# Plain first products in the first block, weight combinations made in the second, and a late half that begins with the weights at hand

## The chip, the core and the metric

The kernel runs on one core of a Trainium2 chip. A core has TensorE (PE; PEld is its weight load), VectorE (DVE), ScalarE (ACT), GpSimd (POOL) and SyncE (SP), which take their instructions in order and wait for one another by semaphores. Here SP issues nearly all loads and POOL the stores. The metric is the device time of one execution in microseconds (us); lower is better.

## What is computed

```python
for t in range(S):                                   # attention: 4 batches, 8 heads, 768 steps, head 64
    state = gamma * state + einsum('bhd,bhe->bhde', k[:, :, t], v[:, :, t])
    y[:, :, t] = scale * einsum('bhd,bhde->bhe', q[:, :, t], state)
x = y.transpose(0, 2, 1, 3).reshape(3072, 512)
h = x @ w_in                                         # layer 0: 512 -> 2048 -> 512
x = np.maximum(0.01 * h, h) @ w_out
h = np.maximum(x @ w_in2, 0.0)                       # layer 1, same sizes
return (h * h) @ w_out2
```

All is float32; weights arrive as 64-bit words and are turned into float32 on the core.

## The kernel before

**Attention.** The 768 steps are three chunks of 256. A unit is one batch and one pair of heads in one chunk: 16 units a chunk. A unit's scores (`sc`) go through a mask on DVE (`pm`), then give its outputs (`y`, copied into `xs` by ACT) and the state's update (`sp`). Chunk 0 runs ahead of everything; one unit of a later chunk is put into each iteration of the early halves and into each of the first steps of the late halves of blocks 0 and 1.

**Layers.** The 3072 rows make three blocks of 1024 per layer: blocks 0, 1, 2 in layer 0 and 3, 4, 5 in layer 1, one after another. A block's 1024 rows are two tiles of 512 columns (t = 0, 1). Each block has an early half with 8 iterations q, which makes the hidden values of both tiles for 256 hidden features per iteration and the second matmuls of tile 0, and a late half, which makes the second matmuls of tile 1 from kept hidden values (`g1`).

**First products.** `emit_in` uses Strassen's scheme as Winograd writes it: the 2x2 block product of weights (`wa`, `wb`: seven combinations) and operands (`xh`, `xl`: seven combinations) takes 7 products instead of 8, at the price of additions on DVE. Every float32 factor is a pair, high and low part, so a product is 6 matmuls of 512 columns (high x high, low x high, high x low, for two halves of the contraction): 42 per iteration. The sums that a product leaves go through ACT (L369 copies, L374 activation) and DVE (L395, L399, L403 add). `split_g` makes the pair `gh`, `gl`.

**Second matmuls.** `emit_out` sends 12 matmuls for each of the 16 slices j of 128 features, into four accumulators, with weights `wo` (two buffers of 1 MB, each for two slices).

**Weights.** In the first block of a layer the weights come raw: `load_w` fetches 1 MB into `sg` (two buffers), `cast` (two ACT, three DVE instructions: L239 to L245) makes float32 in `wf`; `make_in` forms the combinations (L269 to L272), splits them into pairs (`wa`, `wb`) and has POOL store them to DRAM (`wid`), `make_out` the same for `wo` (`wod`). Later blocks read them back (`read_in`: 1 MB and 0.75 MB, `read_out`: 1 MB). In block 2 the odd q of layer 1 are made ahead.

**Order.** Matmuls, loads (SP) and stores (POOL) keep the order of the code. A scheduler at build time sets the order on ACT and DVE by its own estimate of times. PSUM has four accumulators (`ps_acc`), three buffers for products and scores together (`ps_h`), and one for `y`.

Of the kernel before, what the change touches and what calls it, by code (L numbers as in the profile page):

```python
# [40 lines left out]

UNIT = {7: 0, 4: 1, 2: 2, 1: 3, 5: 4, 6: 5, 3: 6}
# [3 lines left out]
def retention_then_two_mlps(  # L46
# [44 lines left out]
    ups = [(c * B + b, p) for c in range(NC) for p in range(NP) for b in range(B)]  # L91
# [128 lines left out]
    wod = {}  # L220
    ydr = {}
    for lay in range(2):
        for q in range(NQ):
            wid[lay, q] = dram.tile([P, 2 * 7 * 256], F32, name=f"wid{lay}_{q}")
            wod[lay, q] = dram.tile([P, 2 * 1024], F32, name=f"wod{lay}_{q}")
    for b in range(NB):
        ydr[b] = dram.tile([P, KB, TB], F32, name=f"ydr{b}")
# [21 lines left out]
    def in_tiles(lay, b, q):  # L249
        ta, tb, bufs = "wa", "wb", (1, 1)  # L250
        pool = w_p
        if q % 2 and late:
            pool = late["p"]
        elif q % 2 and lay == 0 and b == 1:
            ta, tb, bufs = "sg", "wf", (2, 1)
        a = pool.tile([P, 2, 4, 256], F32R, tag=ta, name="wa", bufs=bufs[0])
        c = pool.tile([P, 2, 3, 256], F32R, tag=tb, name="wb", bufs=bufs[1])
        return a, c
# [6 lines left out]
    def make_in(lay, q, ahead=False):  # L265
        load_w(lay, q, 0)
        f = w_p.tile([P, 7, 256], F32, tag="wf", name="wf", bufs=1)
        cast(stage.pop((lay, q, 0)), f[:, 1:5].rearrange("p n c -> p (n c)"))
# [4 lines left out]
        if ahead:  # L273
            a = late["p"].tile([P, 2, 4, 256], F32R, tag="ea", name="ea")
            c = late["p"].tile([P, 2, 3, 256], F32R, tag="eb", name="eb")
        else:
            a, c = in_tiles(lay, 0, q)
        for t, s in ((a, f[:, 3:7]), (c, f[:, 0:3])):
            nc.scalar.copy(t[:, 0], s)
            nc.vector.tensor_tensor(out=t[:, 1], in0=s, in1=t[:, 0].bitcast(F32), op=ALU.subtract)  # L280
# [11 lines left out]
    def get_in(lay, b, q):  # L292
        if b == 0 and (lay == 0 or q % 2 == 0):
            make_in(lay, q)
# [86 lines left out]
    def emit_in(lay, b, q):  # L381
# [7 lines left out]
        late_g = g_p.tile([P, 2, T], F32, tag=f"t{q}", name="g", bufs=1)  # L389
        c22 = g1[j1] = keep(pd, late_g[:, 1])  # L390
        yield
        product(lay, b, q, 6, pa, False, True)
        c12 = g1[j0] = keep(pa, late_g[:, 0])
# [6 lines left out]
        act_sbuf(lay, c22, True)  # L400
        pb = ps_h.tile([P, T], F32, tag="h", name="pb")
# [12 lines left out]


# [3 lines left out]
    halves = {}  # L419

    def split_g(g, tag=None):
# [6 lines left out]
        nc.scalar.copy(gh, g)  # L428
        nc.vector.tensor_tensor(out=gl, in0=g, in1=gh.bitcast(F32), op=ALU.subtract)  # L429
        return gh, gl  # L430

    def emit_out(lay, b, t, j, gg, first=0, end=12):
        if j == 0 and first == 0:
# [3 lines left out]
        gh, gl = gg  # L437
        passes = ((0, gh), (1, gh), (0, gl))
        if j in (0, NJ - 1):
# [3 lines left out]
        for k, m in order[first:end]:  # L443
# [3 lines left out]
                start=j == 0 and k == 0, stop=j == NJ - 1 and k == 2,  # L447
            )

    def evacuate(lay, b, t):  # L450
        ac = acc.pop((lay, b, t))
        dst = ydr[b] if lay == 0 else out[b]
        for m in range(KB):
            if t:
                if m % 2 == 0:
                    yy = g_p.tile([P, 2, T], F32, tag=f"t{4 + m // 2}", name="y", bufs=1)
# [7 lines left out]
            store(out=dst[:, m, t * T:(t + 1) * T], in_=y)  # L464
# [10 lines left out]
    loads_to(1)  # L475
    nc.scalar.dma_start(out=mk[:, 0], in_=mask[:, 0])
    nc.scalar.dma_start(out=vt, in_=vtab)
    loads_to(4)
    nc.scalar.dma_start(out=mk[:, 1], in_=mask[:, 1])
    n0 = B * NP  # L480
    for n in range(n0 + 1):
        if n < n0:
            loads_to(min(n + 5, n0))
            if n in (4, 8):
                nc.scalar.dma_start(out=mk[:, n // 4 + 1], in_=mask[:, n // 4 + 1])
        attend(n0)
        if n == 3:
            make_in(0, 0)
        elif n == 7:
            make_out(0, 0)  # L490
        elif n == 9:
            steps = operands(0, 0)
            next(steps)
            next(steps)
    for _ in steps:
        pass
# [7 lines left out]
    def put_out(lay, b, j):  # L504
        emit_out(lay, b, 0, j, halves.pop(j))

    def split_late(j):
        halves[j] = split_g(g1.pop(j), f"t{j // 2 - 1}" if j % 2 and j > 1 else None)
# [4 lines left out]
    for lay in range(2):  # L513
        for b in range(NB):
# [4 lines left out]
            for q in range(NQ):  # L519
                part = emit_in(lay, b, q)  # L520
                next(part)
                if q:
                    put_out(lay, b, 2 * q - 2)
                next(part)
                if q and q + 1 < NQ:
                    emit_out(lay, b, 0, 2 * q - 1, halves[2 * q - 1], 0, 4)
                if rest:
                    score_next(rest)
                if q and q + 1 < NQ:
                    emit_out(lay, b, 0, 2 * q - 1, halves.pop(2 * q - 1), 4, 12)  # L530
                for _ in part:
                    pass
# [7 lines left out]
                if lay == 0 and b == NB - 1 and q % 2:  # L540
                    make_in(1, q, True)
# [4 lines left out]
            read_out(lay, 0)  # L546
# [3 lines left out]
            read_out(lay, 1)  # L550
            split_late(0)
            split_late(1)
            for j in range(NJ):
                if j + 2 < NJ:
                    split_late(j + 2)
                emit_out(lay, b, 1, j, halves.pop(j))
                if j % 2 == 1 and j + 3 < NJ:
                    read_out(lay, j // 2 + 2)
                if rest and j < 9:
                    attend(rest)  # L560
                if not last and j == 8:
                    steps = operands(nl, nb)
                if not last and j >= 8:
                    next(steps, None)
# [70 lines left out]
```

## Time and profile before

| what | value |
|---|---|
| median of 3 runs | 1198.77 us (1196.65 to 1200.88) |
| the profiled execution | 1199.87 us, its span 1198.1 us |
| busy over the span: PE, PEld, DVE, ACT, POOL | 95%, 74%, 50%, 43%, 4% |
| DMA | 274.57 MB, 229 GB/s in the mean |
| TensorE clock granted, mean | 0.986 of full |

The busy share of PE is counted from modelled ends of matmuls, so it hides short gaps. What tells is the distance between starts, and a comparison of equal stretches of work: the early halves of blocks 0 and 1 send the same matmuls, and so do those of blocks 2 to 5 among themselves, and all late halves of blocks 2 to 5.

### The profile page before, as it was taken

The page shows a single profiled execution, that of the slowest core. Times are in us where ns is not written, and L with a number is a line of the kernel's source. Part 1 is how long each engine was busy: PE and PEld are TensorE (multiplying, and loading weights), DVE is VectorE, ACT ScalarE, POOL GpSimd, SP SyncE. Part 2 cuts the span into 40 slices and gives each one's busy share as a digit, 9 for nine tenths or more (in the row PEclk, how much of TensorE's full clock was granted, in tenths as well). Part 3 has the DMA queues.
Part 4 walks back from the last instruction along what each step waited for, and adds up shares of the span by engine and source line. Part 5 has one row for each costly group of instructions (what it writes and reads, how often), then busy time and mean ns, then how long its engine had stood idle before and what let it go on. Part 6 is the DMA issues. An engine that isn't in the chain of part 4 may idle for free.

```text
span 1198.1 us, 13684 instructions
## 1 busy us (share of the span) xinstructions
PE 1139.0 (95%) x5354; PEld 887.3 (74%) x5354; DVE 598.8 (50%) x875; ACT 515.1 (43%) x812; POOL 52.2 (4%) x100
## 2 busy tenths in 40 slices
PE   8798889999999999999988999999999999999996
PEld 5466666767777776788866878777888878888875
DVE  5986776655222344423486387784233372333331
ACT  3755555423333342244564276763233451433430
POOL 0000000000000000000001010000000000000000
PEclk9979999999999999999999999999999999999998
DMA  9657656755645445578748688856746555755263
GB/s 374 250 204 269 245 219 224 250 204 187 230 177 220 171 162 190 214 247 333 310 178 325 233 319 312 314 201 229 286 185 262 193 177 181 276 194 195 82 213 134
DMA packets 50271, 274.57 MB, mean 229 GB/s; under 512 B 6176, under 2 KB 8224, under 8 KB 26784
## 3 DMA queue, kind: packets, MB, share of 16 engines
q1 hardware_dynamic: 38448, 212.88, 48.6%
q0 software_dynamic: 10752, 58.73, 12.3%
q10 hardware_dynamic: 1008, 2.11, 0.5%
q8 instruction: 42, 0.69, 0.2%
q14 instruction: 21, 0.17, 0.0%
HBM read 214.97 MB, written 58.72 MB: 228 GB/s over the span
## 4 chain that ended last, share of the span: by engine, by line
PE 38%; issue 36%; DMA 13%; DVE 8%; ACT 2%; POOL 1%; SPq 0%; ACTq 0%; POOLq 0%; DVEq 0%
PE acc L83 19%; DMA sg<-w 10%; PE pa L83 8%; PE pd L83 4%; PE y L83 3%; PE sc L83 2%; DMA wo<-wod 2%; PE pb L83 2%; POOL out L89 1%; DVE of L242 1%; DMA mk<-mask 1%; DVE g L395 1%; DMA wb<-wid 1%; DVE wf L242 1%; DVE of L245 1%
## 5 line engine op out<-in xcount | busy, mean ns | idle before, releaser
L83 PE MATMUL acc<-gh,wo 128*128 128x512 f32 x1200 | 313.7, 395 | 11.6 <-DMA wo<-wod 11.0
L83 PEld LDWEIGHTS acc<-gh,wo 128*128 128x128 f32 x1200 | 223.2, 189 | 66.9 <-issue 13.0
L83 PE MATMUL acc<-gl,wo 128*128 128x512 f32 x600 | 171.5, 394 | 0.1
L429 DVE TENSOR_TENSOR gl<-g,gh 128x512 fp32r<-128x512 f32 x150 | 101.7, 689 | 112.8 <-PE acc L83 79.1
L83 PEld LDWEIGHTS acc<-gl,wo 128*128 128x128 f32 x600 | 114.2, 190 | 24.9 <-DVE gl L429 0.6
L83 PE MATMUL pa<-xh,wb 128*128 128x512 f32 x384 | 121.9, 399 | 8.9 <-DVE g L399 6.8
L428 ACT CAST gh<-g 128x512 fp32r<-128x512 f32 x150 | 91.3, 620 | 88.7 <-PE acc L83 85.8
L83 PE MATMUL pa<-xh,wa 128*128 128x512 f32 x384 | 121.5, 398 | 7.2 <-ACT g L369 3.7
L83 PE MATMUL pd<-xh,wa 128*128 128x512 f32 x384 | 120.5, 395 | 4.2 <-ACT g L409 3.0
L83 PE MATMUL acc<-gg,wo 128*128 128x512 f32 x504 | 122.2, 391 | 0.0
L395 DVE TENSOR_TENSOR g<-g,pd 128x512 f32<-128x512 f32 x48 | 33.0, 688 | 164.5 <-PE pd L83 138.5
L83 PEld LDWEIGHTS acc<-gg,wo 128*128 128x128 f32 x504 | 94.2, 188 | 20.2 <-issue 0.7
L369 ACT COPY g<-pa 128x512 f32<-128x512 f32 x96 | 56.4, 587 | 121.3 <-PE pa L83 121.1
L374 ACT ACTIVATE g<-g 128x512 f32<-128x512 f32 x72 | 45.3, 631 | 115.7 <-DVE g L399 65.5
L83 PEld LDWEIGHTS pa<-xh,wb 128*128 128x128 f32 x384 | 71.7, 190 | 30.7 <-DVE g L399 12.3
L83 PEld LDWEIGHTS pa<-xh,wa 128*128 128x128 f32 x384 | 71.1, 189 | 24.3 <-ACT g L369 5.4
L83 PEld LDWEIGHTS pd<-xh,wa 128*128 128x128 f32 x384 | 71.8, 189 | 22.8 <-ACT g L409 5.1
L83 PE MATMUL pa<-xl,wa 128*128 128x512 f32 x192 | 75.6, 394 | 1.8 <-DVE xl L325 1.8
L83 PE MATMUL pa<-xl,wb 128*128 128x512 f32 x192 | 75.6, 394 | 0.0
L83 PE MATMUL pd<-xl,wa 128*128 128x512 f32 x192 | 75.3, 392 | 0.0
L399 DVE TENSOR_TENSOR g<-g,pa 128x512 f32<-128x512 f32 x48 | 32.9, 686 | 71.7 <-PE pa L83 71.6
L83 PE MATMUL pb<-xh,wb 128*128 128x512 f32 x192 | 60.0, 394 | 0.0
(77 smaller groups left out, 1280.3 us busy)
## 6 DMA issues: line engine op xcount, KB each, us to landing
wo<-wod SPq DMA_DIRECT2D x80, 1024.0 KB, 4.8
wa<-wid SPq DMA_DIRECT2D x36, 1024.0 KB, 7.1
sg<-w SPq DMA_DIRECT2D x32, 1024.0 KB, 8.9
wb<-wid SPq DMA_DIRECT2D x36, 768.0 KB, 6.4
wod<-wo POOLq DMA_DIRECT2D x16, 1024.0 KB, 5.6
r<-first SPq DMA_DIRECT2D x48, 256.0 KB, 3.6
wid<-wa POOLq DMA_DIRECT2D x12, 1024.0 KB, 8.3
wid<-wb POOLq DMA_DIRECT2D x12, 768.0 KB, 4.6
```

The lines of the kernel that those rows point to most:

```text
L83: tc.keep_in_program_order(nc.tensor.matmul(**kw))
L89: tc.keep_in_program_order(nc.gpsimd.dma_start(**io))
L242: nc.vector.scalar_tensor_tensor(out=ru, in0=hi, scalar=0x80000000, in1=ru, op0=ALU.bitwise_and, op1=ALU.bitwise_or,)
L245: nc.vector.tensor_tensor(out=ru, in0=ru, in1=lo, op=ALU.add)
L369: nc.scalar.copy(t, ps)
L374: nc.scalar.activation(out=g, in_=g, func=AF.Lrelu)
L395: nc.vector.tensor_tensor(out=c12, in0=c12, in1=pd, op=ALU.add)
L399: nc.vector.tensor_tensor(out=c22, in0=c22, in1=pa, op=ALU.add)
L428: nc.scalar.copy(gh, g)
L429: nc.vector.tensor_tensor(out=gl, in0=g, in1=gh.bitcast(F32), op=ALU.subtract)
```

## The change

- **Block 0** makes its hidden values by plain products (`emit_plain`: 8 products of 6 matmuls, 48 per iteration), straight from the four blocks of the weights (`plain_in`, which casts, splits 4 units instead of 7, and stores the float32 blocks, 0.5 MB, to `wraw`). An activation goes directly from PSUM. The units of chunk 0 are ordered so that tile 0 is complete after 8 units; the two products of q = 0 for tile 0 stand among the last units.
- **Block 1** reads `wraw` (0.5 MB) in place of `wid` and makes the combinations there (`make_in` with lay = 0), storing `wid` for block 2.
- **Layer 1** makes q = 0, 1, 3, 5 ahead (in block 2) and q = 2, 4, 6, 7 in block 3.
- **Late halves** begin with q = 6 and 7 (`LATE`), whose `wo` are still there; the reloads start with q = 0.
- **`emit_in`** has six of the twelve matmuls of slice 2q-1 between its products 7 and 2, and six ahead of the scores, where before four stood ahead and eight behind them.
- **Operand steps** of the next block are spread over the late half, each held behind the latest split.
- The masks 1 to 3 are loaded by SP, and the last outputs are stored by SP.

```diff
+LATE = (6, 7, 0, 1, 2, 3, 4, 5)
+AHEAD = (0, 1, 3, 5)
...
+    ups = [(b, p) for t in range(2) for p in range(NP) for b in (2 * t, 2 * t + 1)]
+    ups += [(c * B + b, p) for c in range(1, NC) for p in range(NP) for b in range(B)]
...
+    def pair_up(t, s):
+        nc.scalar.copy(t[:, 0], s)
+        nc.vector.tensor_tensor(out=t[:, 1], in0=s, in1=t[:, 0].bitcast(F32), op=ALU.subtract)
+
+    def plain_in(q):
+        load_w(0, q, 0)
+        f = w_p.tile([P, 4, 256], F32, tag="wf", name="wf", bufs=1)
+        cast(stage.pop((0, q, 0)), f.rearrange("p n c -> p (n c)"))
+        a = w_p.tile([P, 2, 4, 256], F32R, tag="wa", name="wa", bufs=1)
+        pair_up(a, f)
+        store(out=wraw[q], in_=f.rearrange("p n c -> p (n c)"))
+        win[0, q] = a
+
+    def make_in(lay, b, q, ahead=False):
...
+        if lay == 0:
+            load(out=mid, in_=wraw[q])
+        else:
+            load_w(lay, q, 0)
+            cast(stage.pop((lay, q, 0)), mid)
...
-        if b == 0 and (lay == 0 or q % 2 == 0):
-            make_in(lay, q)
+        if lay == 0 and b == 0:
+            plain_in(q)
+        elif (lay == 0 and b == 1) or (lay == 1 and b == 0 and q not in AHEAD):
+            make_in(lay, b, q)
...
         act_sbuf(lay, c22, True)
+        yield
         pb = ps_h.tile([P, T], F32, tag="h", name="pb")
...
+    def emit_plain(q, i, t):
+        j = 2 * q + i
+        a = win[0, q]
+        ps = ps_h.tile([P, T], F32, tag="h", name="pa")
+        for kb in range(KB):
+            kh, kt = divmod(kb, 2)
+            unit = 2 * (1 - kh) + i if kh == 0 else 1 - i
+            for k, (l, r) in enumerate(((0, 0), (1, 0), (0, 1))):
+                mm(
+                    out=ps, lhsT=a[:, l, unit, kt * P:(kt + 1) * P], rhs=xop[t, kh][r][:, kt],
+                    start=kb == 0 and k == 0, stop=kb == KB - 1 and k == 2,
+                )
...
+        nc.scalar.activation(out=g, in_=ps, func=AF.Lrelu)
+        if t == 0:
+            halves[j] = split_g(g)
...
-            store(out=dst[:, m, t * T:(t + 1) * T], in_=y)
+            put = load if (lay, b, t) == (1, NB - 1, 1) else store
+            put(out=dst[:, m, t * T:(t + 1) * T], in_=y)
...
+                if lay == 0 and b == 0:
+                    if q:
+                        emit_plain(q, 0, 0)
+                        put_out(lay, b, 2 * q - 2)
+                        emit_plain(q, 1, 0)
+                    emit_plain(q, 0, 1)
+                    score_next(rest)
+                    emit_plain(q, 1, 1)
+                    if ahead:
+                        put_out(lay, b, 2 * q - 1)
...
-            for j in range(NJ):
-                if j + 2 < NJ:
-                    split_late(j + 2)
-                emit_out(lay, b, 1, j, halves.pop(j))
-                if j % 2 == 1 and j + 3 < NJ:
-                    read_out(lay, j // 2 + 2)
...
+            for i in range(NJ):
+                if i + 2 < NJ:
+                    split_late(i + 2)
+                emit_out(lay, b, 1, 2 * LATE[i // 2] + i % 2, (0, 12), i == 0, i == NJ - 1)
+                if i % 2 and i // 2 + 2 < NQ:
+                    read_out(lay, LATE[i // 2 + 2])
```

How the order moves, at three places. On DVE, in an iteration in the middle of block 0's early half, before (`of` is the float32 of second weights, `wf` that of first weights):

```order
L241 TENSOR_SCALAR of<-of 128x1024
L242 SCALAR_TENSOR_TENSOR of<-sg,of 128x1024
L245 ISA of<-sg,of 128x2048
L241 TENSOR_SCALAR wf<-wf 128x1024
L242 SCALAR_TENSOR_TENSOR wf<-sg,wf 128x1024
L245 ISA wf<-sg,wf 128x2048
L395 TENSOR_TENSOR g<-g,pd 128x512
```

and the same place now:

```order
L247 TENSOR_SCALAR wf<-wf 128x1024
L248 SCALAR_TENSOR_TENSOR wf<-sg,wf 128x1024
L247 TENSOR_SCALAR of<-of 128x1024
L251 ISA wf<-sg,wf 128x2048
L248 SCALAR_TENSOR_TENSOR of<-sg,of 128x1024
L483 TENSOR_TENSOR gl<-g,gh 128x512
L251 ISA of<-sg,of 128x2048
L149 TENSOR_TENSOR pm<-sc,mk 128x384 x2
L272 TENSOR_TENSOR wa<-wf,wa 128x1024
```

The addition L395, which reads the product's PSUM buffer `pd` and stood behind both casts, is gone; a split and the masks stand behind them now. On DVE in block 1's early half, where before L395, L146, L399, L403, L118 and two L429 made up an iteration, an iteration is now:

```order
L291 TENSOR_TENSOR wf<-wf 128x256
L292 TENSOR_TENSOR wf<-wf 128x256
L293 TENSOR_TENSOR wf<-wf 128x256
L294 TENSOR_TENSOR wf<-wf 128x256
L272 TENSOR_TENSOR wa<-wf,wa 128x1024
L272 TENSOR_TENSOR wb<-wf,wb 128x768
L418 TENSOR_TENSOR g<-g,pd 128x512
L149 TENSOR_TENSOR pm<-sc,mk 128x384 x2
L422 TENSOR_TENSOR g<-g,pa 128x512
L427 TENSOR_TENSOR g<-g,pb 128x512
```

The six instructions for the next iteration's weights came in ahead of L418 (the old L395), and the first of them waits for the load of `wraw`. On SP, from the end of block 2's early half into its late half, before:

```order
L86 DMA wo<-wod_7_101 128x2048
L86 DMA sg<-w 128x1024 x2
L86 DMA wo<-wod_0_87 128x2048
L86 DMA wo<-wod_1_89 128x2048
L86 DMA wo<-wod_2_91 128x2048
```

and now:

```order
L88 DMA wo<-wod_7_101 128x2048
L88 DMA wa<-wid_0_102 128x2048
L88 DMA wb<-wid_0_102 128x1536
L88 DMA sg<-w 128x1024
L88 DMA wo<-wod_0_87 128x2048
L88 DMA wo<-wod_1_89 128x2048
```

One of the two raw loads became a read of layer 1's first weights; the reload of q = 0 is issued two slices into the late half and is wanted two slices after that.

## Rows read from the trace of the kernel before

**Rows 1.** Stretches: us, busy us (x instructions) per engine, PEclk, DMA share, GB/s

```profile
49.70:224.00 174.30, 153.30 (x688) 109.83 (x686) 128.26 (x185) 96.77 (x136) 11.68 (x22) 0.94 0.60 226
299.30:434.30 135.00, 134.13 (x654) 101.29 (x653) 39.22 (x65) 44.76 (x80) 1.50 (x3) 1.00 0.51 191
507.90:625.80 117.90, 113.19 (x494) 92.02 (x493) 56.70 (x77) 58.64 (x89) 4.59 (x9) 1.00 0.72 274
634.00:687.00 53.00, 47.12 (x193) 38.06 (x192) 22.13 (x31) 15.97 (x24) 3.20 (x6) 0.94 0.72 271
687.00:804.30 117.30, 113.95 (x493) 91.73 (x493) 92.95 (x118) 82.45 (x117) 9.93 (x18) 1.00 0.79 299
812.50:857.30 44.80, 44.02 (x194) 35.85 (x194) 15.00 (x20) 12.46 (x20) 2.22 (x5) 1.00 0.65 224
857.30:969.50 112.20, 111.81 (x494) 92.25 (x493) 43.65 (x60) 49.70 (x82) 1.40 (x3) 1.00 0.57 220
60.00:72.20 12.20, 11.28 (x29) 7.95 (x29) 10.73 (x15) 5.22 (x6) 0.07 (x1) 0.51 0.31 109
```

**Rows 2.** Chain that ended last: start us, us, what

```profile
315.37 2.72 PE acc L83 x12
...
333.05 2.72 PE acc L83 x12
...
604.71 13.08 DMA sg<-w
...
648.83 9.18 DMA wo<-wod
```

**Rows 3.** PE in order of time: start us, us, instruction, [idle before <-releaser]

```profile
117.60 0.70 PE L83 MATMUL pa<-xh,wa 128*128 128x512 f32 x2
...
131.16 0.92 PE L83 MATMUL sc<-r 64*128 64x128 f32 x6 [1.22 <-DVE g L395]
...
140.65 0.71 PE L83 MATMUL pa<-xh,wa 128*128 128x512 f32 x2
...
496.87 2.08 PE L83 MATMUL acc<-gh,wo 128*128 128x512 f32 x8 [1.54 <-DMA wo<-wod]
```

**Rows 4.** SP's queue in order of time, block 0

```profile
132.11 0.81 SPq L86 DMA_DIRECT2D r<-first  x2
133.01 0.86 SPq L86 DMA_DIRECT2D sg<-w  x2
```

**Rows 5.** The tile sg in 60 to 230 us: its loads

```profile
DMA to landing us min/median/max: 6.2/9.3/12.6
```

**Rows 6.** ACT in order of time, block 0

```profile
122.79 1.12 ACT L239 ACTIVATE of<-sg 128x1024 f32<-128x1024 f32 x1 [1.37 <-DMA sg<-w]
```

**Rows 7.** DVE in order of time, block 0

```profile
129.16 1.23 DVE L245 CUSTOM_DVE_ANT_0 wf<-sg,wf 128x2048 uint16<-128x2048 uint16 x1
130.42 0.69 DVE L395 TENSOR_TENSOR g<-g,pd 128x512 f32<-128x512 f32 x1
```

**Rows 8.** Waits of the whole span: us in total, times, longest

```profile
PE acc L83 <- DMA wo<-wod: 11.0, 6, 3.9
...
PE sc L83 <- DVE g L395: 7.4, 9, 1.4
...
PE pa L83 <- DVE g L399: 6.8, 13, 1.7
```

**Rows 9.** Groups by shape: busy us, mean ns | idle before

```profile
L395 DVE TENSOR_TENSOR g<-g,pd 128x512 f32<-128x512 f32 x48 | 33.0, 688 | 164.5 <-PE pd L83 138.5 <-ACT g L369 25.6
...
L280 DVE TENSOR_TENSOR wa<-wf,wa 128x1024 fp32r<-128x1024 f32 x12 | 14.7, 1224 | 5.1 <-ACT wa L279 4.9
...
L269 DVE TENSOR_TENSOR wf<-wf 128x256 f32<-128x256 f32 x16 | 6.7, 421 | 0.2
```

**Rows 10.** DMA issues: KB each, median us to landing

```profile
wo<-wod SPq DMA_DIRECT2D x80, 1024.0 KB, 4.8
...
r<-first SPq DMA_DIRECT2D x48, 256.0 KB, 3.6
```

More of the change, by code (lines that the diff above doesn't have):

```diff
@@ L220, in retention_then_two_mlps @@
     wod = {}
+    wraw = {}
     ydr = {}
@@ L225, in retention_then_two_mlps @@
             wod[lay, q] = dram.tile([P, 2 * 1024], F32, name=f"wod{lay}_{q}")
+    for q in range(NQ):
+        wraw[q] = dram.tile([P, 1024], F32, name=f"wraw{q}")
     for b in range(NB):
@@ L436, in emit_out @@
         o = wout[lay, j // 2]
[L437 removed]
+        gh, gl = halves[j]
         passes = ((0, gh), (1, gh), (0, gl))
[L439 removed]
+        if begin or end:
             order = [(k, m) for m in range(KB) for k in range(3)]
@@ L442, in emit_out @@
             order = [(k, m) for k in range(3) for m in range(KB)]
-        for k, m in order[first:end]:
+        for k, m in order[part[0]:part[1]]:
             l, r = passes[k]
@@ L446, in emit_out @@
                 out=ac[m], lhsT=o[:, l, j % 2, m * P:(m + 1) * P], rhs=r,
-                start=j == 0 and k == 0, stop=j == NJ - 1 and k == 2,
+                start=begin and k == 0, stop=end and k == 2,
             )
+        if part[1] == 12:
+            halves.pop(j)
     def evacuate(lay, b, t):
@@ L474, in retention_then_two_mlps @@
         )
-    loads_to(1)
     nc.scalar.dma_start(out=mk[:, 0], in_=mask[:, 0])
     nc.scalar.dma_start(out=vt, in_=vtab)
-    loads_to(4)
-    nc.scalar.dma_start(out=mk[:, 1], in_=mask[:, 1])
     n0 = B * NP
+    for p in range(1, NP):
+        loads_to(2 * p)
+        load(out=mk[:, p], in_=mask[:, p])
     for n in range(n0 + 1):
[L482 to L485, printed above, removed]
+        loads_to(min(n + 6, n0))
         attend(n0)
-        if n == 3:
-            make_in(0, 0)
-        elif n == 7:
+        if n == 2:
+            plain_in(0)
+        elif n == 5:
             make_out(0, 0)
[L491 to L496, printed above, removed]
+        elif n == 8:
+            split_first(0)
+        elif n in (11, 14):
+            emit_plain(0, (n - 11) // 3, 0)
+    split_first(1)
     nc.scalar.dma_start(out=qt, in_=qtab)
@@ L502, in read_x, with put_out, split_late @@
         load(out=xs[NB + b], in_=ydr[b])
[L504 to L508, printed above, removed]
+    def put_out(lay, b, j, part=(0, 12)):
+        emit_out(lay, b, 0, j, part, j == 0, j == NJ - 1)
+    def split_late(i):
+        j = 2 * LATE[i // 2] + i % 2
+        halves[j] = split_g(g1.pop(j), f"t{LATE[i // 2 - 1]}" if i % 2 and i > 1 else None)
     def get_out(lay, b, q):
```

100 lines of the change are left out of this document (55 added, 45 removed).

## Prediction, made blind

> **What bounds the kernel now.** I read the stretches first, because they set equal work side by side [rows 1]. PE is full at full clock in most of them, so PE's own matmuls bound the kernel, and what can be gained is where a stretch is longer than its twin. The early halves of blocks 0 and 1 send the same matmuls and attention units (49.7 to 224.0 and 299.3 to 434.3 us): 174.3 us against 135.0 us, so block 0 loses 39.3 us. Of blocks 2, 3 and 4 (layer 0's last and layer 1's first two) the early halves take 117.9, 117.3 and 112.2 us: 5.7 and 5.1 us lost in blocks 2 and 3. The late half of block 2 takes 53.0 us, that of block 3 44.8 us, which itself holds a short wait: about 9 us lost.
>
> Then the chain: 12 matmuls take 2.72 us, 0.227 us each, and in block 1 the same 12 come again 17.68 us later (315.37 and 333.05), one iteration in which PE hardly waits [rows 2]. In block 0 the first products of two following iterations start 23.05 us apart (117.60 and 140.65) [rows 3]. Why, three queues show together. A score waits for a PSUM buffer that L395 frees (131.16) [rows 3]. When the scores are through, SP issues the next unit's loads (132.11), and only behind them the two raw weight loads (133.01), since its queue is in order [rows 4]. Such a load lands 6.2 to 12.6 us after its issue [rows 5]; ACT starts on the second when it lands (122.79) [rows 6], DVE ends the casts at 130.4, and L395 stands behind them (130.42) [rows 7]; then the next scores run. That is a ring of load, cast, addition and score: 1.8 us of issues (132.11 to 133.87), 12.6 us, 7.6 us (122.8 to 130.4) and 0.7 us give 22.7 us, close to the 23.05 us measured.
>
> **The change, part by part.**
>
> *Plain products in block 0.* 8 iterations with 6 more matmuls are 48 x 0.227 = 10.9 us added. The iteration becomes 17.68 + 6 x 0.227 = 19.04 us if nothing waits. DVE loses four additions of 0.42 us, the split of `wb` (under 1.22 us) and three additions of 0.69 us, about 4.7 us per iteration [rows 9]. More than that counts that L395 leaves the ring: a product's buffer is now freed by one ACT instruction, and no PSUM buffer that the scores need stands behind a cast on DVE. What is left of the ring is load, cast, free `sg` buffer, next load. From the second landing only the cast of the second weights is still to do (two on ACT, three on DVE, a split between them): by the 7.6 us of both casts I take 6.2 us, so 12.6 + 6.2 + 0.4 = 19.2 us with the slowest landing, even with PE's 19.04 us. Landings should be faster than that, since block 0 stores 0.5 MB of `wraw` in place of 1.75 MB of `wid`. I expect PE to set the pace. What remains: at the handover from attention two casts and splits of the second tile, of which part is uncovered, 3 us (two splits of 1.22 us and a little [rows 9]); per iteration between 0 and the 1.2 us that L395 cost [rows 3], so 0.7 us, seven times: 5 us. Sum: -39.3 + 10.9 + 8 = -20.4 us. Part of the 39.3 us is 12.2 us at a granted clock of 0.51 after the handover, half speed, 1.2 GHz [rows 1]; I take it that the shorter gaps keep the full clock.
>
> *Late halves with resident weights.* PE waited six times for `wo`, 11.0 us [rows 8]. One, 1.5 us, is deep in block 1's late half [rows 3], where unit loads share the queue; I leave it. The other five come at the third or later slice, because the reload of the second pair is issued only when the early half has ended. Now four slices of 2.72 us can run first, and each reload is issued 5.4 us ahead of its use, against a median landing of 4.8 us [rows 10]: -9.5 us. In block 2 the two waits are the 3.9 us one [rows 8] and one of 2 us, yet that half is about 9 us long: its clock was 0.94 [rows 1], so some 3 us come back too. I keep 1 us as lost: -11.4 us.
>
> *Block 2's end and block 3.* Of the two raw loads at the end of block 2's early half, one of which took 13.08 us to land [rows 2], one becomes a read of 1.75 MB. ACT still waits for the other with block 2's copies behind it: of 5.7 us I keep 3: -2.7 us. In block 3, L399's waits (6.8 us over the kernel [rows 8]) should go, as 12 matmuls instead of 6 now cover it; against that two `make_in` follow each other at q = 6 and 7, on a DVE that is busy 93 of 117 us [rows 1]. Of 5.1 us I keep 2.6: -2.5 us.
>
> *Combinations in block 1.* Per iteration DVE gets 4 x 0.42 + two splits, at most 2.4 us: about 4 us on a DVE that is busy 39 of 135 us [rows 1, 9]. The cover is PE's 17.68 us. The danger is not the sum but the order: these instructions stand ahead of L418 (the old L395), and the first waits for the load of `wraw`. SP issues it behind the reload of `wo`, which waits for slice 2q-1; that is 54 matmuls and the scores into the iteration, 13.1 us, and three issues of 0.4 us more, so 3.4 us before the next iteration. From its landing to L418 some 5.1 us of splits pass (four additions, two splits, one cast of about a us); L418 is wanted after 36 matmuls, 8.2 us. So it is free up to a landing of 8.2 - 5.1 + 3.4 = 6.5 us. For 0.5 MB the nearest rows are 3.6 us (0.25 MB) and 4.8 us (1 MB) [rows 10]: free. Above lie the landings of the crowded block 0 [rows 5]. Every us beyond 6.5 costs 7 us. I take 2 us of cost, less 1 us for score waits that six matmuls ahead of the scores now cover: +1.0 us. The Trainium skill (TensorE: Matmul & The Clock Gate, the table at its head) gives ScalarE and VectorE a strictly in-order queue. Rows 7 agree, with L395 at 130.42 behind the cast; by that rule alone L418 must wait for every late load, which is the slower rival below.
>
> *The rest.* The masks move to SP with the same bytes, about 0.4 us of issue each, behind which no matmul waits: 0. The last stores leave SP instead of POOL: between 0 and 1 us, -0.5 us. Operand steps hide behind the late halves as before; their price if uncovered is a cast and a split, about 2.3 us, once per block.
>
> Sum: -20.4 - 11.4 - 2.7 - 2.5 + 1.0 - 0.5 = -36.5 us. Against the profiled execution's 1199.87 us (span 1198.1 us), 1.1 us above the median of the runs, that gives **1163 us**.
>
> **Rivals.**
> - *Raw loads still pace block 0.* If the landing stays at 12.6 us and the casts take the whole 7.6 us, with 1.8 us of issues, the ring is 22.0 us and not 19.7 us: six full iterations, 14 us, **1177 us**. For it speaks the ring of today; against it that less is stored and that `wf` is cast before the second load lands.
> - *Reloads merely move the wait.* A landing of 9.18 us against a window of 5.4 us was one wait in block 2 [rows 2], and each reload still has that window. If all waits come back a slice pair later, 11.4 us stay: **1175 us**. Against it: late halves 3 to 5 had one wait each at most, and that at the start.
> - *The clock falls again at the handover.* 12.2 us at 0.51 cost about 6 us: **1169 us**. The Trainium skill (TensorE: Matmul & The Clock Gate, Part 1) says that the slow state is the default and that activity releases it; rows 1 agree with their 0.51, and by it any longer gap at the handover would give that 1169 us.
> - *Block 1 takes over the ring (slower).* If the `wraw` loads land as the slowest of block 0 did, 12.6 us, L418 is 6.1 us late in seven iterations, scores and loads slide with it: +43 us, **1206 us**. From a landing of 11.7 us on the change loses (36.5 / 7 = 5.2 us beyond 6.5). Against it: block 1 moved 191 GB/s at a DMA share of 0.51 [rows 1] and gets only 0.5 MB more per iteration.
>
> **Chances.** The forecast 0.62, raw loads 0.15, moved waits 0.08, the clock 0.08, block 1 0.05, others 0.02. The range 1152 to 1182 us holds the first four: the low end is the forecast without the 8 us and most of the 3 us kept as lost, the high end the raw-load rival and some 5 us of late landings in block 1. Faster or slower by over 0.3% is about what can be told from no change here: faster 0.93, same 0.02, slower 0.05.
>
> **What the next profile would show.** Right: first products in block 0 some 19 to 20 us apart, that early half at about 148 us (5.4 us of its matmuls stand among the attention units) and full clock; PE's wait for `wo` near 2 us in all; block 1's early half within a few us of 135; block 2's late half near 44. Wrong: ACT's L245 waiting for `sg` with PE idle behind it; DVE's L291 waiting for `wf` loads and PE's scores for L418; waits for `wo` at the fifth slice.

## The result, and the profile after

The changed kernel takes **1162.94 us** (median of 4 runs, 1160.83 to 1164.19), the kernel before 1198.62 us (4 runs, 1196.65 to 1200.88): ratio 0.970, 95% interval 0.9676 to 0.9724. The profiled execution took 1160.83 us, its span 1158.8 us. The forecast was 1163 us, but its terms are less good than its sum. Two executions of the experiments, of 2885.79 us (the kernel with the ahead load first) and 1603.48 us (the one with operand steps not held), lie far above the others of the same kernel and are left out of its median and ratio.

The same stretches as [rows 1], of the profile after:

```profile
56.00:68.00 12.00, 11.06 (x58) 7.51 (x57) 9.65 (x14) 5.68 (x9) 1.07 (x2) 1.00 0.64 209
55.70:199.70 144.00, 143.06 (x710) 108.99 (x710) 88.14 (x121) 71.64 (x95) 8.52 (x16) 1.00 0.54 201
275.00:411.00 136.00, 134.88 (x655) 101.42 (x653) 63.72 (x106) 56.17 (x93) 8.97 (x17) 1.00 0.56 210
484.30:596.80 112.50, 111.92 (x494) 92.23 (x493) 45.73 (x66) 49.90 (x80) 4.63 (x9) 1.00 0.75 288
611.30:658.90 47.60, 45.05 (x193) 36.93 (x192) 25.86 (x31) 19.06 (x27) 3.20 (x6) 0.96 0.67 251
658.90:775.60 116.70, 113.98 (x493) 91.81 (x492) 92.22 (x121) 81.54 (x116) 10.97 (x20) 1.00 0.81 310
```

PE fills block 0's early half now (143.06 of 144.0 us, clock 1.00), and the handover ran at 1.00, 2.4 GHz, where it was 0.51 [rows 1]. PE's waits of over 0.15 us in that half add up to 0.9 us, both at the handover; before they were 21.0 us: 5.3 us for the first operand splits, the rest spread over the iterations, mostly for ACT's copies and activations and for L395 and L399. Between the stretches of block 2 stand 14.5 us (596.8 to 611.3) for three slices, 36 matmuls that were 8.2 us before (625.7 to 633.8): the place that became slower (block 1's early half lost 1.0 us besides).

PE in block 0, the first products of three iterations, against 23.05 us apart in [rows 3]:

```profile
85.56 0.71 PE L85 MATMUL pa<-xh,wa 128*128 128x512 f32 x2
...
105.04 0.71 PE L85 MATMUL pa<-xh,wa 128*128 128x512 f32 x2
...
124.52 0.71 PE L85 MATMUL pa<-xh,wa 128*128 128x512 f32 x2
```

They are 19.48 us apart. Of the waits, the lines that answer to [rows 8]:

```profile
ACT wf L245 <- DMA sg<-w: 21.9, 10, 5.8
...
PE acc L85 <- ACT gh L482: 6.0, 5, 4.7
...
PE acc L85 <- DMA wo<-wod: 3.8, 2, 2.5
```

PE's waits for `wo` fell from 11.0 to 3.8 us; those for ScalarE's split (L482, L428 before) grew from 0.7 to 6.0 us, 4.7 of them in one place. The stages, each from the start of its first matmul to that of the next stage (tail: from the last matmul row's start plus 12 x 0.227 us to the end of the span):

| stage, us | before | after | forecast step | measured step |
|---|---|---|---|---|
| end of block 0's early half, from the span's start | 223.95 | 199.72 | -20.4 | -24.2 |
| block 1 early / late | 134.9 / 65.3 | 135.9 / 65.0 | +1.0 | +0.7 |
| block 2 early | 117.8 | 112.5 | | -5.3 |
| block 2, last three slices | 8.2 | 14.5 | -2.7 (both rows) | +6.3 |
| block 2 late | 53.2 | 47.7 | with the next late halves | -5.5 |
| block 3 early | 117.3 | 116.7 | -2.5 | -0.6 |
| late halves 3, 4, 5 together | 135.1 | 130.9 | -11.4 (with block 2's) | -4.2 |
| block 4 early | 112.2 | 111.5 | 0 | -0.7 |
| tail | 10.4 | 4.7 | -0.5 | -5.7 |
| sum | | | -36.5 | -39.2 |

**The new wait, read in four queues of the changed kernel.** SP, in the last iteration of block 2: the raw load `sg` that is prepared ahead is issued behind 1.75 MB of block 3's weights.

```profile
582.42 0.38 SPq L88 DMA_DIRECT2D wa<-wid  x1
584.72 0.32 SPq L88 DMA_DIRECT2D wb<-wid  x1
585.10 0.47 SPq L88 DMA_DIRECT2D sg<-w  x1
616.89 0.32 SPq L88 DMA_DIRECT2D wo<-wod  x1
```

ACT stands for it, with two Lrelu (L397) and the splits behind it; the last addition (L427) that they need had long run on VectorE:

```profile
595.61 0.69 DVE L427 TENSOR_TENSOR g<-g,pb 128x512 f32<-128x512 f32 x1 [0.67 <-PE pb L85]
```

```profile
600.13 1.12 ACT L245 ACTIVATE wf<-sg 128x1024 f32<-128x1024 f32 x1 [5.82 <-DMA sg<-w]
601.15 1.13 ACT L246 ACTIVATE sg<-sg 128x1024 uint32<-128x1024 uint32 x1
602.16 1.15 ACT L397 ACTIVATE g<-g 128x512 f32<-128x512 f32 x2
```

PE's slice 14 therefore waits for `gh`, and the fifth slice of the late half for `wo`:

```profile
604.36 3.42 PE L85 MATMUL acc<-gh,wo 128*128 128x512 f32 x8 [4.71 <-ACT gh L482]
...
624.84 3.40 PE L85 MATMUL acc<-gh,wo 128*128 128x512 f32 x8 [2.55 <-DMA wo<-wod]
```

The load landed 15.0 us after its issue (585.10 to 600.13), and the prepared slice was stored late, on POOL, together with block 2's result, just ahead of the read of `wo` at 616.89:

```profile
612.22 0.53 POOL L91 DMA_DIRECT2D wid<-ea  x1 [26.66 <-DVE ea L272]
612.74 0.53 POOL L91 DMA_DIRECT2D wid<-eb  x1
613.27 2.15 POOL L91 DMA_DIRECT2D ydr<-y  x4
```

The Trainium skill (TensorE: Matmul & The Clock Gate, the table at its head) gives ScalarE a strictly in-order queue; the row at 602.16 agrees, two instructions that had their data by 596.3 (the end of L427) ran only behind the casts, the first of which waited 5.82 us for its load.

### The profile page after: what moved, and what is told of

Same layout as the page of the kernel before. It is cut to its first block, busy times and chain, and to the rows that moved or that the text cites. A ratio compares the mean times of both kernels' runs of the same rounds, so it can differ in the third digit from the quotient of the medians.

```text
span 1158.8 us, 13722 instructions
## 1 busy us (share of the span) xinstructions
PE 1133.4 (98%) x5402; PEld 891.9 (77%) x5402; DVE 587.6 (51%) x852; ACT 508.2 (44%) x793; POOL 54.2 (5%) x104
## 4 chain that ended last, share of the span: by engine, by line
PE 85%; DMA 9%; DVE 3%; ACT 2%; issue 1%; ACTq 0%; SPq 0%; DVEq 0%
PE acc L85 42%; PE pa L85 23%; PE pd L85 8%; DMA sg<-w 4%; PE y L85 4%; PE pb L85 4%; PE sc L85 3%; DMA wa<-wid 1%; DMA wo<-wod 1%; PE sp L85 1%; DMA gt<-gtab 1%; DVE of L248 1%; DMA wf<-wraw 1%; ACT sg L246 0%; DVE of L251 0%
## 5 line engine op out<-in xcount | busy, mean ns | idle before, releaser
L85 PE MATMUL pa<-xh,wa 128*128 128x512 f32 x576 | 181.2, 395 | 2.3 <-DVE wa L272 1.4
L85 PEld LDWEIGHTS pa<-xh,wa 128*128 128x128 f32 x576 | 106.2, 188 | 28.7 <-ACT g L462 2.3
L482 ACT CAST gh<-g 128x512 fp32r<-128x512 f32 x150 | 91.2, 620 | 67.6 <-PE acc L85 66.8
L85 PE MATMUL pa<-xl,wa 128*128 128x512 f32 x288 | 112.5, 391 | 0.3 <-DVE xl L348 0.3
L85 PE MATMUL pa<-xh,wb 128*128 128x512 f32 x320 | 99.6, 393 | 0.5 <-ACT g L392 0.5
L85 PE MATMUL pd<-xh,wa 128*128 128x512 f32 x320 | 98.7, 390 | 0.0
L418 DVE TENSOR_TENSOR g<-g,pd 128x512 f32<-128x512 f32 x40 | 27.5, 687 | 130.5 <-PE pd L85 122.7
L149 DVE TENSOR_TENSOR pm<-sc,mk 128x384 f32<-128x384 f32 x96 | 49.2, 551 | 33.1 <-PE sc L85 30.8
L397 ACT ACTIVATE g<-g 128x512 f32<-128x512 f32 x48 | 30.2, 631 | 79.0 <-DVE g L422 31.8
L85 PEld LDWEIGHTS pa<-xl,wa 128*128 128x128 f32 x288 | 54.0, 188 | 12.3 <-DVE xl L348 0.7
L85 PE MATMUL pa<-xl,wb 128*128 128x512 f32 x160 | 62.3, 389 | 0.0
L85 PE MATMUL pd<-xl,wa 128*128 128x512 f32 x160 | 62.3, 389 | 0.0
```

What stands on the lines that cost most here:

```text
L85: tc.keep_in_program_order(nc.tensor.matmul(**kw))
L149: nc.vector.tensor_tensor(out=t, in0=sc[h][:, 128:512], in1=mk[:, p, h], op=ALU.mult)
L397: nc.scalar.activation(out=g, in_=g, func=AF.Lrelu)
L418: nc.vector.tensor_tensor(out=c12, in0=c12, in1=pd, op=ALU.add)
L482: mark[0] = nc.scalar.copy(gh, g).ins
```

## The experiments

Twelve runs of eleven kernels. Ratios are to the kernel before on the same chip, with 95% intervals; the changed kernel's is 0.970 (0.968 to 0.972), and 0.001 is 1.2 us. Stages are from the one profiled execution of each kernel. Where an edit leaves a stage alone it still differs a little: block 0's first product starts at 35.5 to 39.1 us, and in the changed kernel, the first experiment and the two of block 1 the last three slices of block 2 take 14.5 to 16.2 us and its late half 47.7 to 48.2 us.

**Last stores on POOL (and on SP in the kernel before).** Edit, in one kernel undone and in the other added:

```diff
-            put = load if (lay, b, t) == (1, NB - 1, 1) else store
-            put(out=dst[:, m, t * T:(t + 1) * T], in_=y)
+            store(out=dst[:, m, t * T:(t + 1) * T], in_=y)
```

> The changed kernel with its last four stores back on POOL, as they were in the kernel before; nothing else differs. The prediction's step (the stores' move is worth 0.5 us, since one transfer takes the same time from either queue) expects about 1163.4 us and a tail, from the last matmul to the end of the span, of some 5 us. The theory read from the two traces (a program whose last transfers were issued by POOL ends some 6 us later, though no transfer is running then) expects 1168 to 1169 us and a tail of about 10.4 us, with every stage before the tail as in the changed kernel.

Measured: 1167.84 us, ratio 0.973 (0.971 to 0.976). Its last matmuls and stores, span 1166.6 us:

```profile
1152.48 2.88 PE L85 MATMUL acc<-gg,wo 128*128 128x512 f32 x12
...
1156.38 0.54 POOL L91 DMA_DIRECT2D out<-y  x1 [0.25 <-DVE y L519]
```

and those of the changed kernel, span 1158.8 us:

```profile
1151.34 2.88 PE L85 MATMUL acc<-gg,wo 128*128 128x512 f32 x12
...
1152.84 2.48 SPq L88 DMA_DIRECT2D out<-y  x4
...
1154.26 0.69 DVE L519 COPY y<-acc 128x512 f32<-128x512 f32 x1 [0.67 <-PE acc L85]
```

The tail is 11.4 us against 4.7.

> The kernel before with its last four stores moved from POOL to SP; nothing else differs. If the end of the program is set by which queue issued last, whatever came ahead of it, the time falls by the same 5 to 6 us as in the changed kernel: about 1193 us, tail 4.7 us. If the short tail of the changed kernel came from something else there (less traffic at the end, an earlier last matmul), this kernel stays at 1198 us, tail about 10 us.

Measured: 1191.48 us, ratio 0.993 (0.991 to 0.996), tail 4.0 us. So the four stores are worth 4.9 us in the changed kernel and 7.8 us in the kernel before by the medians (6.7 and 6.4 us by the tails), and the prediction's 0.5 us is wrong. The transfers are not what differs: the four last stores land 2.5 us (median) after their issue from POOL and 2.1 us from SP. The Trainium skill (DMA: Bandwidth & Descriptors, Issuing engines are not separate DMA queues) says that issuing DMAs from several engines saves only the time of the issue, as all run on the same DMA engines; the landings agree. The longer end of the program is not a matter of the transfers.

**The ahead load issued before block 3's weights.**

```diff
                 elif not last:
+                    if lay == 0 and b == NB - 1:
+                        make_in(1, 0, AHEAD[3], True)
                     get_in(nl, nb, 0)
...
-                if lay == 0 and b == NB - 1 and q % 2:
+                if lay == 0 and b == NB - 1 and q % 2 and q + 1 < NQ:
                     make_in(1, 0, AHEAD[q // 2], True)
```

> The changed kernel with one change of order in the last iteration of block 2: the load of the raw weights that are prepared ahead for layer 1 is issued before the reads of block 3's first weights (1.75 MB) and not behind them. Theory: the load stands on SP behind reads that wait for their buffer and then share the transfer engines, so it lands 15 us after its issue, ScalarE stands 5.8 us for it, and the products of slice 14 wait 4.7 us for their operand; with the load ahead, its landing falls to 6 to 8 us, both waits go, block 2's three last slices fall from 14.5 to about 8.5 us, and the time to about 1157 us. Rival: the transfers as a whole are the limit there, the order only changes which of them is late; then the time stays at 1163 us and the reads of block 3's weights or of the next output weights are late in its place.

Measured: **1151.08 us, ratio 0.960 (0.957 to 0.962)**, the fastest version. SP, ACT and POOL at the same place:

```profile
580.47 0.42 SPq L88 DMA_DIRECT2D sg<-w  x1
580.99 0.38 SPq L88 DMA_DIRECT2D wa<-wid  x1
...
610.17 0.32 SPq L88 DMA_DIRECT2D wo<-wod  x1
```

```profile
588.82 1.12 ACT L245 ACTIVATE wf<-sg 128x1024 f32<-128x1024 f32 x1 [2.68 <-DMA sg<-w]
```

```profile
600.26 0.53 POOL L91 DMA_DIRECT2D wid<-ea  x1 [16.61 <-DVE ea L272]
601.73 0.53 POOL L91 DMA_DIRECT2D wid<-eb  x1 [0.94 <-DVE eb L272]
...
605.73 0.54 POOL L91 DMA_DIRECT2D ydr<-y  x1 [0.25 <-DVE y L519]
```

Its three last slices and its late half, as windows (their border is one matmul early: from start to start they are 8.2 and 43.5 us):

```profile
596.40:604.30 7.90, 7.90 (x36) 6.55 (x35) 4.80 (x7) 5.01 (x9) 1.61 (x3) 1.00 0.38 155
604.30:648.10 43.80, 43.80 (x195) 36.26 (x194) 25.42 (x30) 19.36 (x27) 1.62 (x3) 1.00 0.66 246
```

One load, 4.6 us earlier, lands 8.3 us after its issue instead of 15.0. Slices and late half fall from 62.2 to 51.7 us, more than the 6 us expected: the stores of the prepared slice leave POOL 12 us earlier too, 9.9 us ahead of the read of `wo`, which lands after 4.8 us instead of 7.8.

**Late halves in the old order.**

```diff
-LATE = (6, 7, 0, 1, 2, 3, 4, 5)
+LATE = (0, 1, 2, 3, 4, 5, 6, 7)
...
             put_out(lay, b, NJ - 3)
+            read_out(lay, 0)
...
             evacuate(lay, b, 0)
+            read_out(lay, 1)
```

> The changed kernel with the late halves in the old order again (slices 0 to 15, each beginning with a reload of the first two output weights, read at the places where the kernel before reads them). The prediction's step (late halves with resident weights gain 11.4 us, of which 10.0 are seen in the stage table) expects the late halves to lose about 10 us in all, 5.5 of them in block 2, and some 1172 to 1175 us. Rival: other parts of the change (operand steps behind the splits, raw loads out of the way) brought that gain, and the resident weights only moved the wait to the reloads at the end; then the time stays within 3 us of 1163.

Measured: 1165.47 us, ratio 0.972 (0.969 to 0.974), within the rival's 3 us of the changed kernel. Late halves 3, 4 and 5 are 44.75, 46.22 and 44.68 us, together 135.7: the gain of 4.2 us there is gone, so there the prediction's step holds. But block 2's late half is 48.8 us, 1.1 more than in the changed kernel (0.7 to 1.1 by the spread above) and 4.4 less than before. Most of its gain came from another part.

**Slices 1, 3, 5, 7 prepared ahead, as before.** Edit: `AHEAD = (1, 3, 5, 7)`.

> The changed kernel with the slices of layer 1 that are prepared ahead put back to 1, 3, 5 and 7, as in the kernel before (slice 0 is then made from raw weights at block 2's end, beside slice 7). Theory, after the run with the old order of the late halves: block 2's late half lost 9 us because two slices were prepared at block 2's end, whose loads and 3.5 MB of stores met the reads of output weights; so this kernel gets block 2's late half back to 52 to 53 us from 47.7, its end (three slices and late half together) to 61 us or more, block 3's early half to 117 or more, and 1166 to 1172 us in all. Rival (the prediction's step: the resident weights alone made the late half short): block 2's late half stays at 47 to 48 us and the time within 2 us of 1163.

Measured: 1159.81 us, ratio 0.967 (0.964 to 0.970); the profiled execution took 1165.15 us, the longest of its five, and its block 1, which the edit leaves alone, is 2.2 us longer too. The time expected was wrong, the place right: late half 50.7 us (+3.0), block 3's early half 118.7 us (+2.1). But no 1.75 MB stand ahead of the ahead load here, and the three slices take 8.6 us, not 14.5. Two sets of stores leave, one 3 us before the late half (which begins at 610.35) and one in it:

```profile
607.23 0.53 POOL L91 DMA_DIRECT2D wid<-wa  x1 [18.30 <-DVE wa L272]
...
621.34 0.53 POOL L91 DMA_DIRECT2D wid<-ea  x1 [13.06 <-DVE ea L272]
...
622.38 2.14 POOL L91 DMA_DIRECT2D ydr<-y  x4
```

and the `wo` read at 622.12, 0.8 us behind the second set's first store, lands after 9.1 us and is late:

```profile
631.31 3.75 PE L85 MATMUL acc<-gh,wo 128*128 128x512 f32 x8 [3.78 <-DMA wo<-wod]
```

In the kernel before (late half from 633.84) the same two sets left POOL at 631.84 and 645.41, 2.2 and 3.4 us ahead of a read of `wo`: those issued at 634.03 and at 648.83 [rows 2], which landed after 7.3 and 9.2 us and made PE wait 2.0 and 3.9 us:

```profile
631.84 0.53 POOL L89 DMA_DIRECT2D wid<-wa  x1 [24.41 <-DVE wa L280]
...
645.41 0.53 POOL L89 DMA_DIRECT2D wid<-ea  x1 [12.51 <-DVE ea L280]
...
646.46 2.15 POOL L89 DMA_DIRECT2D ydr<-y  x4
```

**Operand steps not held behind the splits.** Edit: `next(steps, None)` without the two `issue_after`. It was run twice; the profile is from the second.

> The changed kernel without the order that keeps the operand steps behind the splits of the late slices; the steps are still written at the same places, but the scheduler may set them ahead. The prediction priced this at nothing: the operand steps hide behind the late halves, a cast and a split of 2.3 us once per block if one is uncovered. It expects 1163 to 1166 us. Rival: the order behind the splits is what keeps late slices from waiting for a split that stands behind a 1.2 us step on VectorE; without it the late halves lose a wait of 1 to 2 us at several slices, 10 us or more in all, 1173 us.

> The same kernel as the run without the order of operand steps behind the splits, taken once more for an undisturbed profile (that run's time was 5 to 7 us above the changed kernel, its profile was of an execution at a low clock). Theory: late slices wait for a gg split that stands on VectorE or ScalarE behind operand steps of 1.05 to 1.2 us, so the late halves are longer by 5 to 7 us together, some 1168 us. Rival: the steps come so early that they delay the last slices of an early half or the copies of accumulators, and the loss shows there.

Measured: 1168.39 us, ratio 0.975 (0.972 to 0.978), and 1167.41 us in the second run, a single execution. Both expectations were partly wrong. The order is worth some 5 us (4.5 and 5.5), not 0; yet late halves 3 to 5 do not change (130.9 us), so the loss expected from late `gg` splits is not there. It lies in small pieces, the largest in block 2: its stores leave POOL at 615.52, 1.8 us ahead of the read of `wo`, which lands after 10.0 us, and the wait grows from 2.55 to 4.75 us (+2.8 us on the late half):

```profile
627.52 3.75 PE L85 MATMUL acc<-gh,wo 128*128 128x512 f32 x8 [4.75 <-DMA wo<-wod]
```

The rest: block 2's early half +1.3, block 3's early half and last slices +2.6, block 4's early half +0.7, block 1's +0.5 us.

**Old places of the odd output slices.**

```diff
-                        put_out(lay, b, 2 * q - 1, (0, 6))
+                        put_out(lay, b, 2 * q - 1, (0, 4))
...
-                    next(part)
                     if ahead:
-                        put_out(lay, b, 2 * q - 1, (6, 12))
+                        put_out(lay, b, 2 * q - 1, (4, 12))
```

(and no yield between products 7 and 2)

> The changed kernel with the 12 matmuls of an odd output slice split 4 ahead of the scores and 8 behind them, as before, and none between products 7 and 2 (the changed kernel: 6 behind product 3, 6 between products 7 and 2). The prediction gave the new places 2.5 us in block 3 (L399's waits) and 1 us in block 1 (score waits). It expects some 3 to 5 us over the changed kernel, 1166 to 1168 us: additions of product 7 that product 2 or 4 waits for, some 0.5 us each, come back in blocks 1, 2, 3 and 4. Rival: the waits were set by VectorE's other work, not by the cover; then within 1 us per block and 1163 us.

Measured: 1158.31 us, ratio 0.967 (0.963 to 0.970): faster than the changed kernel by 4.6 us (the intervals still touch), by neither theory. The new places gain 1.6 us in block 3 (118.3 against 116.7) and nothing in the early halves of blocks 1, 2 and 4 (within 0.2 us). But the three last slices of block 2 take 8.2 us here, because the scheduler put the cast behind the last Lrelu and a split, with a load that still lands 13.4 us after its issue:

```profile
596.44 0.61 ACT L481 CAST gh<-g 128x512 fp32r<-128x512 f32 x1
597.46 1.13 ACT L245 ACTIVATE wf<-sg 128x1024 f32<-128x1024 f32 x1 [0.41 <-DMA sg<-w]
```

With the version that issues the load first this makes two cures for the stall of the slices: the load earlier, or the waiting cast later on its engine. Only the first cures the late half too: here the stores leave at 608.96, 0.8 us ahead of a read of `wo`, PE waits 3.7 us for it, and that half takes 49.1 us.

**The ring in block 0 opened in the kernel before.** Edit, in `load_pair`: the two loads of a unit from the second chunk on are issued by `store` (POOL), not `load` (SP).

> The kernel before with the loads of the raw attention units from the second chunk on moved from SP to POOL, so that the raw weight loads no longer stand behind them on SP; products, casts and combinations are as before. The prediction's ring (load, cast, addition, score, and back to the load by SP's order) is then open: an iteration of block 0 falls from 23.05 us to between 17.7 and 20.2 us (12.6 us of landing and 7.6 us of casts, if the two buffers still chain), its early half from 174 to 150 to 158 us, and the time to 1177 to 1185 us. Rival: VectorE's own queue (casts and combinations of 10 us ahead of the additions) sets block 0's pace, whatever SP does; then the early half stays above 170 us and the time near 1198. Either way the loads on POOL stand behind stores there, which can cost something in blocks 0 and 1.

Measured: 1185.68 us, ratio 0.988 (0.985 to 0.991). The additions that end the ring's turns:

```profile
127.82 0.69 DVE L395 TENSOR_TENSOR g<-g,pd 128x512 f32<-128x512 f32 x1 [0.43 <-ACT g L369]
...
147.11 0.69 DVE L395 TENSOR_TENSOR g<-g,pd 128x512 f32<-128x512 f32 x1 [0.61 <-ACT g L369]
...
167.30 0.69 DVE L395 TENSOR_TENSOR g<-g,pd 128x512 f32<-128x512 f32 x1 [1.40 <-ACT g L369]
```

19.3 and 20.2 us, as expected, and L395 now waits for ACT's copies of the products and no longer for the casts alone. But the iterations before and after took 25.2 and 22.3 us, where a cast waited for a raw load (5.4 us) and the scaling of a unit for its load (2.4 us), with L399 behind them; the early half fell to 166.3 us, 8 us and not 16 to 24; PE's waits in it from 21.0 to 16.2 us. So SP's order did pace block 0, and once it no longer does, late loads pace it through the in-order engines. Most of the rest of the 14 us lies where the edit touches no code: block 2's late half took 48.3 us instead of 53.2 and the tail 7.0 instead of 10.4. That late half thus moves by 5 us without a cause that was looked for.

**Block 1: the saved raw weights made late.** First the load done three times (`for _ in range(3)` round it):

> The changed kernel with the load of the saved raw weights in block 1 done three times in a row into the same tile, each behind the one before; the result is the same. The last lands some 11 us after the first is issued, against 3.7 us for the single one. The prediction's step (free up to a landing of 6.5 us, 7 us for each us beyond it) expects 4 to 5 us beyond, about 30 us on block 1's early half (166 us) and 1193 us. Rival: VectorE's wait for these loads is covered better than the prediction worked out (in the changed kernel it already waits 18.3 us for them and matmuls lose nothing), and the time grows by under 10 us.

Measured: 1166.99 us (2 runs), ratio 0.973 (0.969 to 0.977), block 1's early half 140.0 us, +4.1. A single load lands there after 5.5 to 7.2 us (median 6.2), not the 3.7 us of the expectation. The scheduler set the combinations behind the additions, so the addition never waited for the load: this didn't try the prediction's step, and shows that with another order the weights may land some 14 us after the first issue (326.21 to 339.90 in one turn) for 4.1 us in all. Then two loads, with VectorE's order written out (`keep_in_program_order` on combinations, splits and L418 in block 1):

> The changed kernel with the load of the saved raw weights in block 1 done twice, one behind the other, and with VectorE's order written out there, so that the combinations and splits stay ahead of the first addition as they stand in the changed kernel (where the load was tripled the scheduler had set them behind it, so that run did not try the step). In the changed kernel one such load lands in 6.0 us (median), the addition follows just in time; a second one adds some 5 us. The prediction's step (nothing up to a landing of 6.5 us, 7 us for each us beyond) expects 4 to 5 us beyond in seven iterations: block 1's early half at 165 to 170 us, 1190 to 1196 us in all. Rival: there is more slack than was worked out (other buffers let scores and products run on); then under 10 us.

Measured: **1209.3 us, ratio 1.008 (1.005 to 1.011)**, block 1's early half 183.1 us. It turned the change into a loss, but not by the step as priced. Written out in program order, the combinations of a slice stand at the end of the iteration before it, behind all its additions and splits (L293 at 337.67 for products at 340.48); the scheduler had put them some 10 us sooner (L291 at 328.63 for products at 342.07). PE waits for the weights themselves, 27.0 us in seven waits for the cast L271 and 6.1 us for L272:

```profile
340.48 0.80 PE L85 MATMUL pa<-xh,wa 128*128 128x512 f32 x1 [3.87 <-ACT wa L271]
```

```profile
336.46 1.29 DVE L487 TENSOR_TENSOR gl<-g,gh 128x512 fp32r<-128x512 f32 x2 [0.18 <-ACT gh L486]
337.67 0.42 DVE L293 TENSOR_TENSOR wf<-wf 128x256 f32<-128x256 f32 x1
```

L293 follows the split at once: its data had landed at 327.30, only its place was late. What a late landing costs in the changed kernel's own order was not tried.

**Unit loads on POOL, added to the fastest version.**

> The version with the ahead load issued before block 3's weights (1151 us), and in addition the loads of attention units from the second chunk on moved from SP to POOL. Theory: in block 1 the load of the saved raw weights is then issued about 1 us sooner on SP, so the first addition of a slice no longer ends just when the scores want it: block 1's early half falls from 135.9 to 134.5 or 135 us, the time to about 1150 us. Rival: on POOL those loads stand behind stores that wait for splits, so units come late in blocks 0 and 1, and the time rises above 1152 us.

Measured: 1167.1 us, ratio 0.973 (0.970 to 0.976), 16 us more than without the addition; the rival held. Block 0's early half lost 10 us (172.2 against 162.5 from the same first product) and block 1's 5.6 us, 4.1 of them in one wait of a product for L422. That the unit loads stand behind POOL's stores there is likely, but was not tried apart.

## Why the prediction came out right, and where it did not

- **Plain products, block 0: right, 3.8 us too small.** Interval 19.48 us (19 to 20 said), clock 1.00, early half 144 us (148 said). The ring was real, but opening it alone gives a third of the gain. With the plain products PE's waits went almost altogether (21.0 to 0.9 us), those for L395, L399 and ACT's copies among them (the additions are gone); which share the additions that left VectorE have in that, and which the weights that are cast and not combined, was not tried apart. Of the 8 us kept as lost too much was kept: 0.44 us per iteration, not 0.7, and no slow clock at the handover, so that rival fell.
- **Late halves: the sum nearly right (9.7 of 11.4 us), the cause half right.** In layer 1 the resident weights give the 4.2 us, shown by putting the order back. In block 2 they give at most 1.1 of 5.5 us, little more than the spread there. The two waits for `wo` in it were read as late issues; the runs point to POOL's stores, 1.75 MB of prepared weights and 1 MB of result. Where the first of them leaves 9.9 us ahead of a read, the read lands after 4.8 us and PE does not wait (late half 43.5 us); 4.7 us ahead, it lands after 7.8 us and PE waits 2.55 us; 1.8 us ahead, in the run without the order behind splits, 10.0 and 4.75 us. The time of the stores alone was not varied. They had no term in the sum. The 2.55 us stand at the fifth slice, the place that the prediction named as a sign of being wrong: there the wait had moved, as its second rival said.
- **Block 2's end: wrong in sign.** "ACT still waits for the other with block 2's copies behind it: of 5.7 us I keep 3" names the mechanism; the size failed: early half and slices together lost 1.0 us instead of gaining 2.7. In the kernel before, the stall behind the load of 604.71 [rows 2] hit the last products (PE waits of 2.02 and 1.71 us at 619.45 and 624.17), now it hits the slices. ACT's L245 waiting for `sg` with PE idle behind it, a sign named for block 0, showed here. The step missed that the read which replaces one raw load is issued ahead of the other, so that this one lands at 15.0 us.
- **Block 3: 0.6 instead of 2.5 us.** The new places of the odd slices give 1.6 us (118.3 to 116.7), so something else in the change costs 1.0 us (117.3 before, 118.3 with the old places). That it is the shifted slices is not shown: with the old slices the half took 118.7 us, 2.1 us more and not less.
- **Block 1: right in size**, +1.0 us of the early half, but from other terms. The 1 us that the new places were to give back is not there (135.7 us with the old ones, 135.9 with the new), so the cost was 1.0 us, not 2; and the 7 us for each us beyond 6.5 was not tried by any run. VectorE waited 18.3 us for these loads, one of the signs named as wrong, but PE waited only 0.9 us for L418. One turn shows how near it is: the load issued at 321.43 is waited for until 328.63, 7.2 us, a little over the 6.5 us said to be free, and L418 runs at 333.44, just when the scores want it.

```profile
321.43 0.78 SPq L88 DMA_DIRECT2D wf<-wraw  x1
```

```profile
328.63 0.43 DVE L291 TENSOR_TENSOR wf<-wf 128x256 f32<-128x256 f32 x1 [3.35 <-DMA wf<-wraw]
...
333.44 0.68 DVE L418 TENSOR_TENSOR g<-g,pd 128x512 f32<-128x512 f32 x1
```

- **The rest: wrong by 5.2 us for the last stores.** The term for the last stores, "between 0 and 1 us", had no row behind it; the end of the program was not looked at, though the trace of the kernel before had the last store's issue (1188.86) and the span's end (1198.1) to read. And the operand steps, said to hide as before, were hidden by the order that the change gave them, worth some 5 us.

So the forecast hit because block 0 (3.8), the last stores (5.2) and block 4 (0.7) made up for block 2's end (3.7), block 3 (1.9) and the late halves (1.7). The hit to 0.1 us is luck: the sum was taken from a profiled execution 1.1 us above its median and is compared with a median, while the profiled executions themselves fell by 39.0 us (1199.87 to 1160.83), 2.5 more than the sum.

## What to carry to other kernels

Where a load feeds work that is prepared ahead, issue it before the reads that are needed later, even if those look more urgent: here one load, 4.6 us earlier in SP's in-order queue, was worth 12 us by the medians (10.5 us in the stages behind it), a third of this whole change. When a late wait is a DMA's, look also at what other queues stored in the microseconds before, and at what made those stores late. Undo the parts one by one even when the sum fits: five terms of this one were off by 1.7 to 5.2 us, in both directions.

## What the runs showed of the hardware that was not expected

- The program ended 7.0, 10.4 and 11.4 us after its last matmul where POOL issued the last four stores (the opened ring, the kernel before, the first experiment), and 4.0 to 5.0 us after it where SP did. After the last bytes of the outputs had moved it ran on for 3.4, 6.9 and 7.8 us with POOL, and for 1.4 to 2.4 us with SP (the kernel before with SP, the changed kernel, the fastest version). Why POOL ends later, and why less so in the opened ring, was not found out.
- A stall costs more than its length: behind waits of 4.71 and 2.55 us the next 8 matmuls took 3.42 and 3.40 us where they take 1.98, 1.4 us more each time. The granted clock fell to the lower level (1.2 GHz) for most of these stretches, 0.58 and 0.56 in the mean, after PE had stood; the same 8 matmuls of the slice before ran at 1.00 (596.77 to 598.60).

```profile
604.36:607.80 3.44, 3.44 (x9) 2.77 (x10) 3.37 (x8) 1.30 (x2) 0.00 (x0) 0.58 0.00 0
624.84:628.10 3.26, 3.26 (x9) 2.60 (x10) 0.45 (x1) 0.00 (x0) 0.00 (x0) 0.56 0.50 211
```
